# Three sets of four channel tiles by seven half products in block 6, and the sums of u queued behind the preceding block's last adds

## The chip, the cores and the metric

The kernel runs on one core of one Trainium2 chip. The metric is the device time of one execution in microseconds (us), lower is better. Engines are named as in the profile: PE (matrix products), DVE, ACT and POOL (elementwise work), SP (a queue that issues DMAs and DMA transposes). POOL issues DMAs too, the loads of q, k and v.

## The reference

Causal attention over 8 batches of 8 heads, 576 tokens and 16 beacon tokens in front, then a mixer over tokens of low rank, then two dense layers with a ReLU between them and a residual.

```
x = attention(q, k, v, beacon_k, beacon_v)        # B=8, S=576, H*D=512
h = x^T @ U @ V                                   # over tokens, rank 32
u = x + h^T
out = u + max(u @ w_ch1, 0) @ w_ch2               # 512 -> 2048 -> 512
```

## The kernel before

**Tiling.** Attention works on pairs of heads: pair `p` belongs to batch `p // 4`. Scores go to tiles `sps`, ACT turns them into weights (`expt`, by exp), DVE masks them against `bigmask`, PE makes the weighted sum `po`, DVE normalises it into `xb` (`rec`, then a multiply). When a batch is whole, its tokens are transposed into `uT` and the low-rank term is added. The two dense layers work on 9 blocks of 512 tokens, numbered 0 to 8, which run through batches: 4608 rows in all. A block is a list of units that goes into `queue`, and `fill(n)` takes n units from it between the pieces of attention. So a block's matmuls and the attention of a later batch alternate on PE, in an order that is written out by hand (`long_slot`), and blocks 7 and 8 run alone at the end. Every engine keeps the order in which the program emits its instructions.

**Layer 1** of a block makes 16 channel tiles of `gT` (128 channels by 512 tokens each). A plain tile (`layer_one`) is four matmuls of 512 columns into a bank `gps`, then a ReLU on ACT or DVE. A *set* (`quad` in the code) is four tiles, two of the lower eight and two of the upper eight, made at once by a scheme of Strassen's kind: seven half products in place of eight, each of four matmuls of 256 columns. `step(q, n)` emits set q in four steps, n = 0 to 3. It has a bank `qpsA` that gathers a running sum; after steps 0, 1 and 2 ACT copies that sum out (`copied`, into `kept` or a piece of a staging tile), and the next product of `qpsA` may start only when the copy has been taken. A second bank `qpsD` gathers too; after step 2 DVE adds it to a copy (`summed`), and only then may step 3 add its product to `qpsD`. A third, `qpsF`, is used within step 0. The set needs sums of pieces of w1 (`quad_weights`, four POOL instructions of 128x512, once) and sums of pieces of u (`u_sums`, four DVE instructions of 128x512 per block: t1 to t4, which lie in the last 512 columns of the four staging tiles `st`).

**Layer 2** is seven products of the same kind (`products`, banks `mpsA` to `mpsF`), each in two units (`c_unit`), and `after(k)` takes product k out of its bank with a DVE add; for the products on `mpsE` and at last on `mpsD` that add makes an output tile `ob`, to which POOL adds u (`residual`) before SP stores it. `ahead(n)` emits the sums of u of the next block within the last units of layer 2, one sum a unit from unit 10 on (`AHEAD`).

**Who uses what.** `PARTS` says how many sets a block makes: none in blocks 0 to 2, one in 3 to 6, three in 7 and 8 (`quads`). The four staging tiles hold q and k of a batch as loaded: `qk_tiles` gives even batches the first two and odd batches the other two; from batch 4 on (`DT0`) they are loaded by `load_whole` and brought into `kT` and `qT` by DMA transposes on SP (`turns`), one batch ahead. `coming` holds loads and weight builds that wait for their turn: each unit taken from `queue` lets one of them go to POOL. `pst` gives out the eight PSUM banks in the order in which they were emptied.

Of the kernel before, what the change touches and what calls it, by code (L numbers as in the profile page):

```python
# [11 lines left out]
F32 = mybir.dt.float32  # L12
# [18 lines left out]
def kernel(  # L31
# [14 lines left out]
    B, H, S, D = q.shape  # L46
# [6 lines left out]
    NH2 = H // 2  # L53
# [199 lines left out]

    def qk_tiles(b=0):

        t = staged[2 * (b % 2) : 2 * (b % 2) + 2]
        st = [x[:, :].rearrange("p (h e) -> p h e", h=H) for x in t]
        whole = [x[:, 0 : NT * DM].rearrange("p (j h d) -> p j h d", h=H, d=D) for x in t]
        return st, whole
# [311 lines left out]
    def quad_tiles(q):  # L571

        if q == 0:
            w = [pairs.tile([P, 512], F16, name=f"lw{k}", tag=f"pr{k % 2}") for k in range(4)]
        else:
            w = [staged[q - 1][:, ds(512 * k, 512)] for k in range(4)]
            f = staged[q + 1][:, 0 : 2048].bitcast(F32).rearrange("p (k i x) -> p k i x", k=2, i=2)
            lq["k", q] = (f[:, 0], f[:, 1], f[:, 0])
        lq["w", q] = [x.rearrange("p (c f) -> p c f", c=2) for x in w]

# [31 lines left out]
    def fast_units(t0, dst, last=False, parts=0, ahead=None):  # L612


        cell, banks, obs = {}, {}, {}
        quads = parts > 1
        cols = u_cols(t0, 512)

        def begin():
# [39 lines left out]
        def layer_one(dc, on_vector, between=lambda: None):  # L659

            g = pst([P, 512], F32, name="gps")
            for cc in range(NCC):
                for at, o, w in cols:
                    nc.tensor.matmul(  # L664
                        g[:, ds(o, w)], w1[:, cc, ts(dc, P)], uT[:, cc, ds(at, w)],
                        start=(cc == 0 and o == 0), stop=(cc == NCC - 1), skip_group_check=len(cols) > 1,
                    )
            between()
            if on_vector:
                nc.vector.tensor_scalar_max(out=cell["g"][:, dc, :], in0=g, scalar1=0.0)  # L670
            else:
                nc.scalar.activation(out=cell["g"][:, dc, :], in_=g, func=AF.Relu)  # L672
            emptying(g)

        def g_quads():
# [4 lines left out]
            held = {}  # L680

            def plain(k, dc):
                layer_one(dc, not quads and k in (2, 11, 13))

            def half(q, bank, a, b, fresh):
                if fresh:
# [32 lines left out]
            def step(q, n):  # L719
                d, e = 2 * q, HF + 2 * q  # L720
                if n == 0:
                    half(q, "A", of_w1(0, d), b11, True)
                    copied(q, 0)
                    half(q, "F", of_w1(2, d), b21, True)
                    summed(q, "F", 0, d, 0)
                    emptying(held.pop((q, "F")))
                    relu(cell["g"][:, ds(d, 2), 0:HT])
                elif n == 1:
                    half(q, "A", of_lw(q, 1), t2, False)
                    copied(q, 1)  # L730
                    half(q, "D", of_lw(q, 0), t1, True)
                elif n == 2:
                    half(q, "A", of_lw(q, 2), t3, False)
                    copied(q, 2)
                    summed(q, "D", 2, e, HT)
                else:
                    half(q, "A", of_w1(2, e), t4, False)
                    nc.scalar.activation(out=cell["g"][:, ds(e, 2), 0:HT], in_=held[q, "A"], func=AF.Relu)
                    emptying(held.pop((q, "A")))
                    half(q, "D", of_lw(q, 3), b22, False)  # L740
                    summed(q, "D", 1, d, HT)
                    emptying(held.pop((q, "D")))
                    relu(cell["g"][:, :, HT:512].rearrange("p (h d) t -> p h d t", h=2)[:, :, ds(d, 2), :])

            if not quads:
                slots = [2, (0, 0), 10, (0, 1), 3, 11, (0, 2), 4, (0, 3), 12, 5, 13, 6, 14, 7, 15]
                late = {11: ((0, 0, 4),), 12: ((1, 0, 4),), 13: ((2, 0, 4),), 14: ((0, 4, 3),), 15: ((1, 4, 3),)}
# [35 lines left out]

        after_g = {0: ((0, 6, 2), (1, 6, 2)), 1: ((2, 0, 4),), 4: ((2, 4, 4),), 6: ((3, 0, 4),), 7: ((3, 4, 4),)}
        sums_at = {k - NDC: x for k, x in SUMS.items()}
        if parts:
            sums_at = {0: ((2, 4, 3),), 1: ((0, 7, 1), (1, 7, 1)), 2: ((2, 7, 1), (3, 0, 4)), 3: ((3, 4, 4),)}

        b11, b21, b22 = w2[:, 0:HF, 0:HC], w2[:, HF:NDC, 0:HC], w2[:, HF:NDC, HC:DM]
# [112 lines left out]
        def c_unit(k, j):  # L902
            p = pieces(products[k][0])[j]
            if parts and k < 2:
                (first, second_on)[k](*p)
            else:
                product(*products[k], *p)
            for x in sums_at.get(2 * k + j, ()):
                sums(*x)
            for u in ahead(2 * k + j) if ahead else ():  # L910
                u()
            if j == 1 and not (parts and k < 2):
                after(k)

        def chain_units():

# [296 lines left out]
    DT0 = 4  # L1213
    LAG = 10
    HINT = 5
    FAST = 1
    PARTS = {3: 1, 4: 1, 5: 1, 6: 1, 7: 3, 8: 3}
    AHEAD = 10
    SUMS = {
# [27 lines left out]

    def sums_ahead(t):

        if PARTS.get(t, 0) != 1:  # L1250
# [64 lines left out]
    with tc.manual_schedule(engines={ENG.PE, ENG.Activation, ENG.DVE, ENG.SP, ENG.Pool}):  # L1315
# [186 lines left out]

        for p in range(NP1, NP):
            b, c = divmod(p, NH2)
            if c == (1 if b >= DT0 else 0) and b + 1 < B:
                load_batch(b + 1)
            if p == P6 + 3:
                quad_tiles(0)
                coming.extend(quad_weights(0))
            if p == NP - 3:  # L1510
                for n in (1, 2):
                    quad_tiles(n)
                    coming.extend(quad_weights(n))
            if c == (1 if b + 1 == DT0 else 2) and DT0 <= b + 2 < B:
                load_whole(b + 2)
            qk = qkT_of(p + 2) if P6 <= p and p + 2 < min(NP, DT0 * NH2) else []
            if p == P6:
                turn_x(b - 1)
                mix_between(b - 1)
            if c == 0 and DT0 <= b + 1 < B:  # L1520
                tr = turns(b + 1)
                fill_turns(tr, len(tr))
            if p < P6:
                play(third[c])
            else:
                long_slot(p, c, av_of(p), qk or [lambda: None] * 2)
# [109 lines left out]
```

## Time and profile before

| what | value |
| --- | --- |
| time, median of 3 runs | 334.12 us (333.8 to 334.57) |
| the profiled execution's own time, its span | 334.53 us, 332.9 us |
| PE, DVE, ACT, POOL busy | 324.4, 264.9, 195.8, 149.3 us |
| layer 1 of block 6 on PE | 249.01 to 265.16 us |
| layer 2 of block 6 | 265.16 to 278.46 us |
| layer 1 of block 7 (three sets, no attention beside it) | 278.46 to 291.12 us |

The time from a row of a timeline is its start in the span, then the time from its first start to its last end; "x8" means eight instructions that follow each other. Ends of matmuls are modelled, so the step from one start to the next says what a matmul costs on PE. A pair in brackets is the idle time ahead of the instruction and what ended it.

### The profile page before, as it was taken

To read this page: it belongs to the slowest core of one execution; us is meant where nothing else is said; L and a number is where in the kernel's file an instruction comes from. 1 tells how busy PE (TensorE), PEld (TensorE's weight loads), DVE (VectorE), ACT (ScalarE), POOL (GpSimd) and SP (SyncE) were. 2 spreads that over 40 slices of the span, in tenths; PEclk is the share of its full clock that TensorE was granted. 3 is DMA by queue.
4 is the path that set the end of the run, shared out by engine and by line. 5 is a ranking of instruction groups with operands and counts; after the bars stand their busy time and mean duration, and the time that the engine had idled before them with its cause. 6 is when DMAs were issued, how large, how long until landed. Compare 5 with 4: busy or idle time off the path is not lost.

```text
span 332.9 us, 9194 instructions
## 1 busy us (share of the span) xinstructions
PE 324.4 (97%) x3646; PEld 226.9 (68%) x3646; DVE 264.9 (80%) x600; ACT 195.8 (59%) x429; POOL 149.3 (45%) x185
## 2 busy tenths in 40 slices
PE   7999999999999999999999999999999999999994
PEld 3665555555578655876588888764886588788784
DVE  6685888678898667796789777887799858898993
ACT  5966971688972577347844695379535413713710
POOL 8986824657147950669046903360294014010010
PEclk9999999999999999999999999999999999999999
DMA  7999999999999995999989995964204413205013
GB/s 161 143 165 153 177 188 199 193 188 170 79 128 165 208 140 76 130 184 145 124 146 181 141 147 104 129 143 109 41 33 142 77 46 109 51 32 141 20 36 101
DMA packets 150562, 41.99 MB, mean 126 GB/s; under 512 B 131312, under 2 KB 149936, under 8 KB 150512
## 3 DMA queue, kind: packets, MB, share of 16 engines
q0 software_dynamic: 87568, 18.18, 75.0%
q1 hardware_dynamic: 62144, 22.41, 35.4%
q10 hardware_dynamic: 800, 0.75, 0.7%
q8 instruction: 30, 0.49, 0.6%
q14 instruction: 20, 0.16, 0.2%
HBM read 37.45 MB, written 9.44 MB: 141 GB/s over the span
## 4 chain that ended last, share of the span: by engine, by line
PE 86%; DVE 6%; ACT 5%; DMA 1%; issue 1%; DVEq 0%
PE gps L664 21%; PE mpsA L880 8%; PE po L428 8%; PE sps L410 6%; PE mpsD L800 5%; PE qpsA L690 5%; PE cps L1019 4%; PE gps L993 4%; PE mpsB L800 3%; PE mpsE L800 3%; PE mpsC L800 3%; PE qpsD L690 3%; PE mpsF L800 2%; PE mpsD L880 2%; ACT expt L377 2%; ACT w L377 2%
## 5 line engine op out<-in xcount | busy, mean ns | idle before, releaser
L419 ACT ACTIVATE expt<-sps 128x496 f16<-128x496 f32 (+2 forms) x192 | 82.2, 546 | 43.7 <-PE sps L410 43.7
L820 POOL TENSOR_TENSOR ob<-ob,ut 128x512 f32<-128x512 f32 x26 | 31.9, 1230 | 137.5 <-DVE ob L820 66.1
L664 PE MATMUL gps<-uT,w 128*128 128x512 f16 (+1 forms) x400 | 84.9, 354 | 0.2 <-ACT kT L1145 0.2
L800 PEld LDWEIGHTS <-gT 128*128 128x128 f16 x576 | 54.3, 98 | 8.7 <-issue 2.6
L664 PEld LDWEIGHTS <-w 128*128 128x128 f16 x400 | 36.6, 98 | 29.0 <-issue 1.8
L672 ACT ACTIVATE gT<-gps 128x512 f16<-128x512 f32 x68 | 40.6, 618 | 19.6 <-PE gps L664 14.1
L642 DVE TENSOR_TENSOR gT<-gT 128x1024 f16<-128x1024 f16 (+3 forms) x90 | 47.3, 550 | 0.9
L239 POOL DMA_DIRECT2D vs<-in_v_dram x50 | 40.0, 813 | 14.8 <-DMA w<-in_moe_w_ch_dram 12.0
L428 PEld LDWEIGHTS <-expt 128*128 128x128 f16 x900 | 33.8, 98 | 8.5 <-issue 1.5
L428 PE MATMUL po<-vs,expt 128*128 128x65 f16 x900 | 36.4, 194 | 0.3
L349 DVE TENSOR_TENSOR expt<-expt,bigmask 128x768 f16<-128x768 f16 x54 | 34.5, 679 | 0.4 <-ACT expt L419 0.2
L880 PEld LDWEIGHTS <-gT 128*128 128x128 f16 x336 | 31.2, 98 | 4.2
L437 DVE TENSOR_TENSOR xb<-po,rec 128x320 f16<-128x320 f32 x64 | 31.4, 491 | 2.2
L709 ACT ACTIVATE kept<-qpsA 128x512 f32<-128x512 f32 x18 | 10.8, 602 | 22.6 <-PE qpsA L690 12.0
L410 PE MATMUL sps<-qT,kT 64*128 64x80 f16 (+4 forms) x288 | 22.9, 281 | 0.2 <-DVE ob L820 0.2
L670 DVE TENSOR_SCALAR gT<-gps 128x512 f16<-128x512 f32 x20 | 13.8, 689 | 11.4 <-PE gps L664 11.3
L436 DVE RECIPROCAL rec<-po 128x5 f32<-128x5 f32 x64 | 12.0, 188 | 12.1 <-PE po L428 11.7
L377 ACT ACTIVATE expt<-sps 128x496 f16<-128x496 f32 (+2 forms) x48 | 20.5, 556 | 1.3 <-PE sps L371 1.3
L410 PEld LDWEIGHTS <-kT 64*128 64x128 f16 x288 | 10.3, 94 | 13.2 <-issue 8.6
L880 PE MATMUL mpsA<-w,gT 128*128 128x256 f16 x160 | 19.0, 273 | 0.0
L1092 POOL DMA_DIRECT2D st<-in_k_dram x20 | 16.9, 859 | 1.3 <-DVE qT L332 1.3
L1092 POOL DMA_DIRECT2D st<-in_q_dram x20 | 16.9, 875 | 0.0
(159 smaller groups left out, 519.1 us busy)
## 6 DMA issues: line engine op xcount, KB each, us to landing
out_dram<-ob SPq DMA_DIRECT2D x33, 256.0 KB, 3.2
vs<-in_v_dram POOLq DMA_DIRECT2D x18, 128.0 KB, 7.1
w<-in_moe_w_ch_dram POOLq DMA_DIRECT2D x4, 512.0 KB, 6.8
w<-in_moe_w_ch_dram POOLq DMA_DIRECT2D x2, 1024.0 KB, 12.9
st<-in_k_dram POOLq DMA_DIRECT2D x12, 128.0 KB, 6.2
st<-in_q_dram POOLq DMA_DIRECT2D x12, 128.0 KB, 7.6
st<-in_k_dram POOLq DMA_DIRECT2D x4, 288.0 KB, 12.0
st<-in_q_dram POOLq DMA_DIRECT2D x4, 288.0 KB, 12.8
```

Source lines behind the costliest of these rows:

```text
L239: nc.gpsimd.dma_start(out=dst[a : a + nq[j], j, :, :], in_=src[hs, ds(q0[j], nq[j]), :].rearrange("h p d -> p h d"))
L349: nc.vector.tensor_tensor(out=e, in0=e, in1=bigmask[:, :, :].rearrange("p (a b) x -> p a b x", b=2), op=ALU.min)
L377: nc.scalar.activation(out=ex[i][:, ds(AT[g], gw[g])], in_=ps[g, i][:, 0 : gw[g]], func=AF.Exp, scale=scale)
L410: nc.tensor.matmul(banks[i][:, ds(at0 + o, w)], kT(hp, c, ch), qT[hp, c, ds(qa, w)], start=True, stop=True, skip_group_check=len(unit) > 1,)
L419: nc.scalar.activation(out=at[p][3][i][:, ds(AT[g], gw[g])], in_=bank[:, ds(at0, gw[g])], func=AF.Exp, scale=scale)
L428: nc.tensor.matmul(po[:, j, :], ex[0 : nk[c], ds(blk[(c, j)], P)], vs[0 : nk[c], ds(c * H * E + h * E, E)], start=(c == 0), stop=(c == j),)
L642: nc.vector.tensor_tensor(out=o[:, ds(d0, n)], in0=x[:, ds(d0, n)], in1=y[:, ds(d0, n)], op=op)
L664: nc.tensor.matmul(g[:, ds(o, w)], w1[:, cc, ts(dc, P)], uT[:, cc, ds(at, w)], start=(cc == 0 and o == 0), stop=(cc == NCC - 1), skip_grou ...
L672: nc.scalar.activation(out=cell["g"][:, dc, :], in_=g, func=AF.Relu)
L800: nc.tensor.matmul(ps, a()[:, d, ds(P * i, P)], bm[:, d, ds(c0, w)], start=fresh and d == 0 and i == 0, stop=d == HF - 1, skip_group_check ...
L880: nc.tensor.matmul(ps, a()[:, d, ds(P * i, P)], bm[:, d, ds(c0, w)], start=fresh and d == 0, stop=d == HF - 1, skip_group_check=True,)
L1092: coming.append(lambda d=dst, s=src, a=m[j] - nq[j], n=m[j], j=j: nc.gpsimd.dma_start(out=d[a:n, j, :, :], in_=s[:, ds(q0[j], nq[j]), :].r ...
```

## The change

Block 6 makes three sets and four plain tiles in layer 1 instead of one set and twelve plain tiles. Its order of units is new, the bank `qpsD` of sets 1 and 2 is begun a step later than that of set 0, and the sums that layer 2 needs are emitted mostly in layer 2. For that the w1 sums of set 1 are built by POOL in the second pair of batch 4 instead of at the end of batch 7, and live in the third staging tile; the copies of set 1 go to the first. That takes the third and fourth staging tile from the batches, so all batches from 4 on are loaded into the first two, and batch 5 is loaded one pair later. Last, in layer 2 of every block of this kind `after(k)` is emitted ahead of `ahead(n)`, so that a sum of u stands behind the add of the same unit instead of ahead of it.

```diff
     def qk_tiles(b=0):
-        t = staged[2 * (b % 2) : 2 * (b % 2) + 2]
+        i = 2 * (b % 2) if b < DT0 else 0
+        t = staged[i : i + 2]
...
-            w = [staged[q - 1][:, ds(512 * k, 512)] for k in range(4)]
-            f = staged[q + 1][:, 0 : 2048].bitcast(F32).rearrange("p (k i x) -> p k i x", k=2, i=2)
+            w = [staged[q + 1][:, ds(512 * k, 512)] for k in range(4)]
+            f = staged[q - 1][:, 0 : 2048].bitcast(F32).rearrange("p (k i x) -> p k i x", k=2, i=2)
...
-        quads = parts > 1
+        quads = t0 // 512 >= NBLK - 2
...
-                layer_one(dc, not quads and k in (2, 11, 13))
+                layer_one(dc, parts == 1 and k in (2, 11, 13))
...
+                elif n == 1 and parts > 1 and not quads:
+                    if q == 0:
+                        half(q, "D", of_lw(q, 0), t1, True)
+                    half(q, "A", of_lw(q, 1), t2, False)
+                    copied(q, 1)
...
                     copied(q, 2)
+                    if q and not quads:
+                        half(q, "D", of_lw(q, 0), t1, True)
                     summed(q, "D", 2, e, HT)
...
-                slots = [2, (0, 0), 10, (0, 1), 3, 11, (0, 2), 4, (0, 3), 12, 5, 13, 6, 14, 7, 15]
+                if parts > 1:
+                    slots = [
+                        (0, 0), (0, 1), 6, (0, 2), (1, 0), (0, 3), (1, 1), 14, (1, 2), (2, 0), (1, 3), (2, 1), 7,
+                        (2, 2), 15, (2, 3),
+                    ]
+                    late = {12: ((0, 0, 4),), 14: ((1, 0, 4),)}
...
-        if parts:
+        if parts > 1:
+            sums_at = {
+                0: ((0, 4, 4),), 1: ((1, 4, 4),), 2: ((2, 0, 4),), 3: ((2, 4, 4),), 4: ((3, 0, 4),), 5: ((3, 4, 4),),
+            }
+        elif parts:
...
+            if j == 1 and not (parts and k < 2):
+                after(k)
             for u in ahead(2 * k + j) if ahead else ():
                 u()
-            if j == 1 and not (parts and k < 2):
-                after(k)
...
-    PARTS = {3: 1, 4: 1, 5: 1, 6: 1, 7: 3, 8: 3}
+    PARTS = {3: 1, 4: 1, 5: 1, 6: 3, 7: 3, 8: 3}
...
+            if p == P6 + NH2 + 1:
+                quad_tiles(1)
+                coming.extend(quad_weights(1))
...
-                for n in (1, 2):
-                    quad_tiles(n)
-                    coming.extend(quad_weights(n))
-            if c == (1 if b + 1 == DT0 else 2) and DT0 <= b + 2 < B:
+                quad_tiles(2)
+                coming.extend(quad_weights(2))
+            if c == 2 and DT0 <= b + 2 < B:
                 load_whole(b + 2)
```

On DVE, where layer 2 of block 5 ends (`st_113` to `st_116` are written with t1 to t4 of block 6, `expt` is masked for the two heads whose weighted sums come next). Before:

```order
L820 TENSOR_TENSOR ob<-mpsD,kept 128x512
L593 TENSOR_TENSOR st_113<-uT 128x512
L593 TENSOR_TENSOR st_114<-uT,st_113 128x512
L820 TENSOR_TENSOR ob<-mpsE,kept 128x512
L349 TENSOR_TENSOR expt_105<-expt_105,bigmask 128x3x2x128
L349 TENSOR_TENSOR expt_106<-expt_106,bigmask 128x3x2x128
L593 TENSOR_TENSOR st_115<-uT 128x512
L593 TENSOR_TENSOR st_116<-uT,st_114 128x512
L820 TENSOR_TENSOR ob<-mpsD,kept 128x512
```

The same place of DVE with the change:

```order
L839 TENSOR_TENSOR ob<-mpsD,kept 128x512
L594 TENSOR_TENSOR st_113<-uT 128x512
L839 TENSOR_TENSOR ob<-mpsE,kept 128x512
L594 TENSOR_TENSOR st_114<-uT,st_113 128x512
L350 TENSOR_TENSOR expt_105<-expt_105,bigmask 128x3x2x128
L350 TENSOR_TENSOR expt_106<-expt_106,bigmask 128x3x2x128
L594 TENSOR_TENSOR st_115<-uT 128x512
L839 TENSOR_TENSOR ob<-mpsD,kept 128x512
L594 TENSOR_TENSOR st_116<-uT,st_114 128x512
```

The second sum now stands between the add of `mpsE` and the two masks, and the last add stands ahead of the fourth sum. The same rows stand at the ends of blocks 2, 3 and 4.

On ACT in layer 1 of block 6 (a row with `gps` is a plain tile's ReLU, one with `kept<-qpsA` or `st<-qpsA` is the copy of a set's running sum, `gT<-qpsA` its last ReLU, `expt` the exp of scores). Before:

```order
L672 ACTIVATE gT<-gps 128x512
L709 ACTIVATE kept<-qpsA 128x512
L419 ACTIVATE expt_107<-sps_4849 128x496
L419 ACTIVATE expt_108<-sps_4850 128x496
L709 ACTIVATE kept<-qpsA 128x512
L672 ACTIVATE gT<-gps 128x512 x2
L709 ACTIVATE kept<-qpsA 128x512
L672 ACTIVATE gT<-gps 128x512
L738 ACTIVATE gT<-qpsA 128x2x256
L672 ACTIVATE gT<-gps 128x512 x5
```

The same place of ACT with the change:

```order
L710 ACTIVATE kept<-qpsA 128x512 x2
L673 ACTIVATE gT<-gps 128x512
L420 ACTIVATE expt_107<-sps_4854 128x496
L420 ACTIVATE expt_108<-sps_4855 128x496
L710 ACTIVATE kept<-qpsA 128x512
L710 ACTIVATE st_113<-qpsA 128x512
L746 ACTIVATE gT<-qpsA 128x2x256
L710 ACTIVATE st_113<-qpsA 128x512
L673 ACTIVATE gT<-gps 128x512
L710 ACTIVATE st_113<-qpsA 128x512
L710 ACTIVATE st_114<-qpsA 128x512
L746 ACTIVATE gT<-qpsA 128x2x256
```

Before, the second copy of the one set stood behind the two exps. Now it is the third copy of set 0, with a plain tile's ReLU ahead of the exps, and the copies of set 1 follow it.

On POOL, in the part of the program that belongs to batch 4 (`lw` are the w1 sums of set 0, those into `st_115` the w1 sums of set 1, `vs` loads of v, `ob` the residual of an output tile), with the change:

```order
L1111 DMA st_114<-in_q_dram 80x8x64
L606 TENSOR_TENSOR lw_2404<-w_93 128x512
L606 TENSOR_TENSOR lw_2405<-lw_2404,w_93 128x512
L606 TENSOR_TENSOR lw_2406<-w_93 128x512
L606 TENSOR_TENSOR lw_2407<-w_93,lw_2405 128x512
L606 TENSOR_TENSOR st_115<-w_93 128x512
L839 TENSOR_TENSOR ob<-ob,ut 128x512
L606 TENSOR_TENSOR st_115<-st_115,w_93 128x512
L606 TENSOR_TENSOR st_115<-w_93 128x512
L606 TENSOR_TENSOR st_115<-w_93,st_115 128x512
L221 DMA vs_112<-in_beacon_v_dram 16x8x64
```

Before, `lw_2412<-w_93,lw_2410` was followed at once by the load of `vs_112`, and the eight sums of sets 1 and 2 stood together near the end of batch 7.

More of the change, by code (lines that the diff above doesn't have):

```diff
@@ L745, in g_quads @@
             if not quads:
-                slots = [2, (0, 0), 10, (0, 1), 3, 11, (0, 2), 4, (0, 3), 12, 5, 13, 6, 14, 7, 15]
-                late = {11: ((0, 0, 4),), 12: ((1, 0, 4),), 13: ((2, 0, 4),), 14: ((0, 4, 3),), 15: ((1, 4, 3),)}
+                if parts > 1:
[4 more added lines that the diff above has]
+                    late = {12: ((0, 0, 4),), 14: ((1, 0, 4),)}
+                else:
+                    slots = [2, (0, 0), 10, (0, 1), 3, 11, (0, 2), 4, (0, 3), 12, 5, 13, 6, 14, 7, 15]
+                    late = {11: ((0, 0, 4),), 12: ((1, 0, 4),), 13: ((2, 0, 4),), 14: ((0, 4, 3),), 15: ((1, 4, 3),)}
                 def unit(k, slot):
@@ L1248, in sums_ahead @@
     def sums_ahead(t):
-        if PARTS.get(t, 0) != 1:
+        if t not in PARTS or t >= NBLK - 2:
             return None
```

## The prediction

> **What bounds the kernel now.** I read the page first, for shares and clock.
>
> ```profile
> span 332.9 us, 9194 instructions
> PE 324.4 (97%) x3646; PEld 226.9 (68%) x3646; DVE 264.9 (80%) x600; ACT 195.8 (59%) x429; POOL 149.3 (45%) x185
> PE 86%; DVE 6%; ACT 5%; DMA 1%; issue 1%; DVEq 0%
> ```
>
> PE is busy for 97% of the span, and 86% of the chain that ended last is PE. So an edit is worth what it takes from PE's stream, plus the waits in that stream that it ends, less those that it makes. A windows view gives the stretches that matter: layer 1 of block 6, then layer 1 of block 7, which already makes three sets (columns: length, busy time of PE, PEld, DVE, ACT, POOL, then clock, DMA share, GB/s).
>
> ```profile
> 249.01:265.16 16.15, 15.98 (x145) 9.48 (x142) 13.90 (x27) 8.04 (x15) 3.98 (x3) 1.00 0.48 106
> 278.46:291.12 12.66, 12.66 (x102) 9.71 (x100) 10.63 (x21) 8.63 (x15) 1.72 (x2) 1.00 0.39 106
> ```
>
> PE runs at full clock in both. In block 6 it has a hole, and DVE is busy for 13.90 of 16.15 us: it is second. PE's timeline shows the hole between a plain tile and the scores behind it; the two rows after the dots are the same place in block 5.
>
> ```profile
> 251.66 1.03 PE L664 MATMUL gps<-uT,w 128*128 128x512 f16 x4
> 252.62 0.31 PE L410 MATMUL sps<-qT,kT 64*128 64x336 f16 x1
> 253.10 0.37 PE L410 MATMUL sps<-qT,kT 64*128 64x336 f16 x5 [0.17 <-DVE ob L820]
> ...
> 218.44 0.60 PE L410 MATMUL sps<-qT,kT 64*128 64x336 f16 x8
> 218.97 0.61 PE L690 MATMUL qpsA<-st,lw 128*128 128x256 f16 x4
> ```
>
> From the first score matmul to the second, 0.48 us pass. In block 5 eight of them take 0.53 us together, 0.07 each on average, so about 0.45 us are a wait, more than the 0.17 in brackets, since modelled ends cover the rest. What PE waits for is DVE's last `ob` add of block 5, which frees a bank. DVE and POOL show why it was late:
>
> ```profile
> 247.87 0.68 DVE L820 TENSOR_TENSOR ob<-mpsE,kept 128x512 f32<-128x512 f32 x1
> 248.47 2.34 DVE L349 TENSOR_TENSOR expt<-expt,bigmask 128x768 f16<-128x768 f16 x2
> 250.73 1.38 DVE L593 TENSOR_TENSOR st<-uT 128x512 f16<-128x512 f16 x1
> 252.04 0.41 DVE L593 TENSOR_TENSOR st<-uT,st 128x512 f16<-128x512 f16 x1
> 252.37 0.68 DVE L820 TENSOR_TENSOR ob<-mpsD,kept 128x512 f32<-128x512 f32 x1
> ...
> 248.93 1.47 POOL L605 TENSOR_TENSOR st<-w,st 128x512 f16<-128x512 f16 x1
> 250.36 1.47 POOL L820 TENSOR_TENSOR ob<-ob,ut 128x512 f32<-128x512 f32 x1
> ```
>
> The same DVE instruction takes 0.41 us at 252.04 and 1.38 us at 250.73. The long one lies over a POOL instruction. POOL is then building w1 sums and adding residuals.
>
> **The change, part by part.** *Fewer columns.* A matmul's price is the step between starts in block 7:
>
> ```profile
> 283.74 0.60 PE L690 MATMUL qpsA<-st,lw 128*128 128x256 f16 x4
> 284.18 1.04 PE L690 MATMUL qpsA<-st,st 128*128 128x256 f16 x8
> 285.05 1.89 PE L664 MATMUL gps<-uT,w 128*128 128x512 f16 x8
> 286.78 0.49 PE L690 MATMUL qpsA<-st,w 128*128 128x256 f16 x3
> ```
>
> Twelve of 256 columns take 285.05 - 283.74 = 1.31 us, 0.109 each; eight of 512 take 1.73 us, 0.216 each. Four plain tiles are 16 x 0.216 = 3.46 us, a set is 28 x 0.109 = 3.05 us. Two sets more save **0.82 us**. This lies on the path whole. The Trainium skill speaks against it ("TensorE: Matmul & The Clock Gate", Back-to-back issue gap): a stream of weight loads and matmuls runs at about 81 ns for 128 columns and 131 ns for 512. On a line between these, an estimate from that page, 256 columns cost 98 ns, and a set of 2.73 us would be dearer than four tiles of 2.10 us: the sum's first term would be +1.3 us. The rows above disagree with that, and they decide.
>
> *The wait at 252.62.* With the change four of POOL's eight late builds are gone from there, and the last add stands ahead of a sum. I take the wait as gone: **-0.45 us**. What is late next is below.
>
> *A new wait of PE for ACT.* By the order of ACT in block 6, PE's units after the first plain tile are six score matmuls, step 2 of set 0, step 0 of set 1, step 3 of set 0. Step 3 needs the copy from step 2, and that copy stands behind a ReLU and two exps. ACT's rows (the last two from block 6 before):
>
> ```profile
> 284.38 0.60 ACT L709 ACTIVATE kept<-qpsA 128x512 f32<-128x512 f32 x1 [0.28 <-PE qpsA L690]
> 284.87 1.08 ACT L709 ACTIVATE st<-qpsA 128x512 f32<-128x512 f32 x2
> 286.11 0.60 ACT L672 ACTIVATE gT<-gps 128x512 f16<-128x512 f32 x1 [0.16 <-PE gps L664]
> 253.49 1.06 ACT L419 ACTIVATE expt<-sps 128x496 f16<-128x496 f32 x2 [1.92 <-PE sps L410]
> 254.43 0.60 ACT L709 ACTIVATE kept<-qpsA 128x512 f32<-128x512 f32 x1
> ```
>
> The plain tile's matmuls that began at 285.05 end their turn at 285.92; its ReLU starts 0.19 later. The next instruction follows 0.49 after a ReLU or copy (284.38 to 284.87), two exps take 0.94 (253.49 to 254.43), a copy 0.60. So the copy is done 0.19 + 0.49 + 0.94 + 0.60 = 2.22 us after the tile. PE meanwhile has six scores (0.53 less two of 496 columns at 0.11 each, about 0.31), four matmuls of step 2 (0.44) and eight of step 0 (0.87): 1.62. It waits **+0.60 us**. In the old order two plain tiles lay in that gap.
>
> *A wait for DVE behind it.* Step 3's second product needs the DVE add of step 2, which needs the same copy.
>
> ```profile
> 256.71 0.59 ACT L709 ACTIVATE kept<-qpsA 128x512 f32<-128x512 f32 x1
> 257.34 0.69 DVE L712 TENSOR_TENSOR gT<-qpsD,kept 128x512 f16<-128x512 f32 x1 [0.57 <-ACT kept L709]
> ```
>
> The add starts 0.04 after the copy and takes 0.69: 0.73 us, with 0.44 of PE's step 3 beside it. Wait: **+0.30 us**. The like places of sets 1 and 2 have cover. Behind step 2 of set 1 lie a weighted sum and step 0 of set 2, behind that of set 2 a plain tile of 0.87 us, which covers copy (0.60) and add (0.69) only with the first product's 0.44 as well. I put **+0.10 us** there, between 0 and 0.3.
>
> *The sums of u.* The second sum now delays the masks of the next two heads by 0.41 us at the ends of blocks 2 to 5. Block 4's start shows what that meets:
>
> ```profile
> 179.66 1.98 DVE L349 TENSOR_TENSOR expt<-expt,bigmask 128x768 f16<-128x768 f16 x2
> 180.12 1.51 DVE L349 TENSOR_TENSOR expt<-expt,bigmask 128x768 f16<-128x768 f16 x1
> 179.82 1.40 POOL L820 TENSOR_TENSOR ob<-ob,ut 128x512 f32<-128x512 f32 x1 [1.26 <-DVE ob L820]
> 181.40 0.61 PE L428 MATMUL po<-vs,expt 128*128 128x65 f16 x15
> 219.17 4.01 POOL L820 TENSOR_TENSOR ob<-ob,ut 128x512 f32<-128x512 f32 x3 [8.49 <-DVE xb L437]
> ```
>
> The first mask runs before POOL's residual of the same output tile, the second waits for it and ends at 181.63, 0.41 after POOL. With the sum in front, the first mask is the one that waits. POOL starts when the sum is done, 179.66 + 0.41 = 180.07, 0.13 earlier than before, so the mask ends near 181.5, and the weighted sum due at 181.40 waits; with the weight load between, about 0.2 us, from 0 to 0.45. The Trainium skill has this as a rule ("SBUF — State Buffer", Who interferes with whom): DVE with two inputs from SBUF and a POOL instruction that reads SBUF hold a shared port as an exclusive lock, and issue order decides who blocks. By that rule the order that the change makes is the worse one, and these rows agree. Block 5 is spared: POOL stands still there until 219.17. Block 6 meets it, since with POOL's builds gone its residual falls as in block 4. Block 3 may, but POOL is then behind with the moved loads and builds; I count 0 there. Two places: **+0.40 us**.
>
> *Loads and builds.* Batch 5 is loaded a pair later, and four builds of 1.16 us each stand in POOL ahead of v of that batch.
>
> ```profile
> st<-in_q_dram POOLq DMA_DIRECT2D x12, 128.0 KB, 7.6
> 109.61 1.80 POOL L1092 DMA_DIRECT2D st<-in_q_dram  x2
> 131.30 2.30 SPq L1108 DMA_TRANSPOSE kT<-st  x1
> ```
>
> Before, POOL issued loads of q from 109.61 on, 0.9 us each. In the new order nine loads stand behind a residual that came after all of them, at about 115; so the last is issued near 123, an estimate, and lands 7.6 later, near 131, as the transposes of batch 5 begin. Batch 5 is scored two pairs after these. I put 0 here; without that cover SP would hold stores and transposes for a microsecond or two.
>
> *Sum*, against the profiled execution's own 334.53 us (332.9 of span, 1.63 around it): -0.82 - 0.45 + 0.60 + 0.30 + 0.10 + 0.40 = +0.13. That execution is 0.41 above the median of the runs, so I add 0.13 to the median of 334.12: 334.25, written **334.3**. A measurement of this kernel tells about 0.2%, 0.67 us, from no change, so the forecast is no change within that.
>
> **The rivals.** *A: the copy does not hold PE.* For it: block 7 makes three sets in 12.66 us with PE busy throughout, and gains of 1.27 us would then stand alone: 334.12 - 1.27 = 332.9. Against it: block 7 has no exps, and the 0.60 comes from fixed orders on two engines. Chance 0.12; over half of the new waits must vanish to be faster by 0.2%.
>
> *B: DVE is still late.* The rows behind its last `ob` add price the adds and weighted sums that follow:
>
> ```profile
> 252.97 0.18 DVE L436 RECIPROCAL rec<-po 128x5 f32<-128x5 f32 x1
> 253.59 0.68 DVE L712 TENSOR_TENSOR gT<-qpsF,kept 128x512 f16<-128x512 f32 x1
> 254.31 0.29 DVE L717 TENSOR_SCALAR gT<-gT 128x512 f16<-128x512 f16 x1
> 254.52 0.18 DVE L436 RECIPROCAL rec<-po 128x5 f32<-128x5 f32 x1
> ```
>
> By starts, a weighted sum's two instructions take 0.62, an add with its ReLU 0.72 + 0.21. The second mask ends some 1.5 us into block 6 (the first 1.0 in, as in block 4, the second half a microsecond later); two sums of u at 0.33 (252.04 to 252.37), the `ob` add at 0.60, add and ReLU, two weighted sums: 1.5 + 0.66 + 0.60 + 0.93 + 1.24 = 4.9. The add behind the copy is due later: PE's work ahead of the first plain tile is as long as before, the tile starts at 251.66 and ends 0.87 on, the copy is done 2.22 after that, 5.7 us into the block. So DVE has 0.8 us in hand. Before, its last `ob` add began 3.4 us into the block, in my count 1.8. If it stays those 1.6 us late, the 0.45 stays and the add is 0.8 late, less where the waits overlap: 334.25 + 0.95 = 335.2, an estimate. For it: 13.90 busy of 16.15, six adds more, and the port. Against: half of POOL's builds leave. Chance 0.25.
>
> *C: half products do not overlap as full ones do.* At their full rows a group of four costs 0.60 (283.74) and a plain tile 1.03 (251.66): a set of 4.20 against four tiles of 4.12, so two sets lose 0.16 in place of gaining 0.82, and the time is 334.25 + 0.82 + 0.16 = 335.2. The skill's gap figures above point this way. The twelve in 1.31 us, in a block of sets alone, speak against it. Chance 0.02.
>
> *D: late loads hold SP*, 1 to 2 us, chance 0.03.
>
> **How the numbers follow.** The forecast has 0.58, of which 0.56 lie within 0.2% and 0.01 on either side. Of B's 0.25, 0.23 are slower by more than that. Faster: 0.12 + 0.01 = 0.13. Slower: 0.01 + 0.23 + 0.02 + 0.03 = 0.29. Same: the rest, 0.58. The range goes from half-way to A, 333.4, to just beyond B, 335.4.
>
> **What would show it.** Right: PE's timeline in block 6 with a hole of about 0.6 us ahead of step 3 of set 0, ended by ACT's `kept`, and one of 0.3 ended by DVE; no hole at the scores; a hole of 0.2 at the first `po` of blocks 4 and 6; layer 1 of block 6 about 16.0 us long. Wrong: layer 1 of block 6 at 15.0 us (A), DVE's last `ob` add more than 3 us into it (B), or a wait on SP's transposes near 131 us (D).

## The result, and the profile after

The changed kernel takes 335.76 us (median of 9 runs, 335.08 to 336.83), the kernel before beside it 334.25 us (9 runs, 333.80 to 334.76). The ratio is 1.0047, 95% interval 1.0035 to 1.0059: slower by 1.5 us, where the forecast was 0.13 us and the range ended at 335.4. The profiled execution took 335.72 us, that of the kernel before 334.53. Medians are over all runs; ratios and intervals leave out the few runs in the chip's slower state.

From the page of the changed kernel, the span, the engines' shares and the chain that ended last:

```profile
span 334.0 us, 9275 instructions
PE 324.9 (97%) x3670; PEld 228.6 (68%) x3670; DVE 266.2 (80%) x604; ACT 197.4 (59%) x432; POOL 149.3 (45%) x185
PE 87%; ACT 6%; DVE 3%; DMA 1%; issue 1%; ACTq 0%; DVEq 0%
```

DVE's part of the chain fell from 6% to 3%, and yet the span grew. So shares don't show it; stretches do. The windows view of layer 1 of blocks 6 and 7 (length, busy time of PE, PEld, DVE, ACT, POOL, then clock, DMA share, GB/s):

```profile
249.85:265.75 15.90, 15.38 (x169) 11.65 (x166) 14.40 (x30) 9.70 (x19) 1.83 (x2) 1.00 0.37 91
279.05:291.71 12.66, 12.66 (x102) 9.70 (x100) 10.62 (x21) 8.64 (x15) 1.72 (x2) 1.00 0.40 106
```

Block 6, where the new sets are, got shorter: 15.90 us, 16.15 before. Its rows on PE, then ACT, then DVE show the forecast's steps one by one:

```profile
252.68 1.03 PE L665 MATMUL gps<-uT,w 128*128 128x512 f16 x4
253.64 0.39 PE L411 MATMUL sps<-qT,kT 64*128 64x336 f16 x6
253.96 0.61 PE L691 MATMUL qpsA<-st,lw 128*128 128x256 f16 x4
...
254.85 0.60 PE L691 MATMUL qpsF<-uT,w 128*128 128x256 f16 x4
255.84 0.60 PE L691 MATMUL qpsA<-st,w 128*128 128x256 f16 x4 [0.39 <-ACT kept L710]
256.56 0.60 PE L691 MATMUL qpsD<-uT,lw 128*128 128x256 f16 x4
...
254.24 1.05 ACT L420 ACTIVATE expt<-sps 128x496 f16<-128x496 f32 x2
255.17 0.62 ACT L710 ACTIVATE kept<-qpsA 128x512 f32<-128x512 f32 x1
...
255.82 0.69 DVE L713 TENSOR_TENSOR gT<-qpsD,kept 128x512 f16<-128x512 f32 x1 [0.84 <-ACT kept L710]
```

The six scores at 253.64 follow at once: no hole there. Four matmuls of 256 columns take 0.44, so step 3 of set 0 was due at 255.29 and starts at 255.84, 0.55 late, behind ACT's copy; its second product was due at 256.28 and starts at 256.56, 0.28 late, behind DVE's add.

So the loss lies ahead of block 6. I took the start of each matmul in both traces and subtracted; the difference is flat nearly everywhere and steps at a few places. The table gives the steps for the changed kernel and for every experiment (us, by which PE falls back against the trace of before; "po" is a block's first weighted sum, "plain" the plain tile behind the scores; layer 1 of block 6 includes its own first `po`).

| kernel | po, block 3 | plain, block 3 | po, block 4 | plain, block 4 | scores, block 5 | layer 1, block 6 | elsewhere after 100 us |
|---|---|---|---|---|---|---|---|
| changed | 0.76 | 0.11 | 0.17 | 0.16 | 0.29 | -0.25 | 0 |
| e1 order only | 0.18 | 0.16 | 0.17 | 0.16 | 0 | +0.31 | 0 |
| e10 second sum only | 0.18 | 0 | 0.17 | 0 | 0 | +0.31 | 0 |
| e11 fourth sum only | 0 | 0 | 0 | 0 | 0 | -0.34 | 0 |
| e3 loads only | 0 | 0.03 | 0 | 0 | 0 | -0.47 | 0.19 at 158 |
| e2 old order | 0 | 0.06 | 0 | 0 | 0 | -0.42 | 0.19 at 157 |
| e6 change, builds later | 0.18 | 0.17 | 0.17 | 0.16 | 0 | -0.25 | 0.44 at 162 |
| e7 no residual | 0 | 0 | 0 | 0 | 0 | -0.42 | 0.09 at 158 |
| e8 sum behind masks | 0 | 0.72 | 0 | 0.33 | 0 | -0.42 | 0 |
| e4 new slots | 0 | 0.31 | 0 | 0 | 0.79 | -1.19 | 0.09, 0.19 |
| e5 and builds later | 0 | 0 | 0 | 0 | 0 | -1.19 | 0.62 at 162 |
| e9 and builds split | 0 | 0 | 0 | 0 | 0 | -1.20 | 0.51 at 192 |
| e12 split, earlier | 0 | 0 | 0 | 0 | 0 | -1.19 | 1.20 at 124 |

In the changed kernel blocks 3 to 5 lose 1.49 and block 6 gains 0.25: a loss of 1.24 us, where the medians are 1.5 apart and the two profiled executions 1.19. (In the first 20 us the other traces are 0.32 to 1.00 ahead of before's, whatever the kernel, e3's loses 0.47 again before 60 us, and behind the last matmul they lose 0.05 to 1.38; none of this is put down to a change.)

The largest step, on PE, DVE and POOL at block 3; the last three rows are PE and DVE at the same place before:

```profile
145.69 1.03 PE L665 MATMUL gps<-uT,w 128*128 128x512 f16 x4
147.31 0.62 PE L429 MATMUL po<-vs,expt 128*128 128x65 f16 x15 [0.59 <-DVE expt L350]
...
144.82 0.41 DVE L594 TENSOR_TENSOR st<-uT,st 128x512 f16<-128x512 f16 x1
145.16 2.57 DVE L350 TENSOR_TENSOR expt<-expt,bigmask 128x768 f16<-128x768 f16 x2
...
143.85 1.79 POOL L239 DMA_DIRECT2D vs<-in_v_dram  x2
145.66 1.17 POOL L839 TENSOR_TENSOR ob<-ob,ut 128x512 f32<-128x512 f32 x1
...
146.34 1.03 PE L664 MATMUL gps<-uT,w 128*128 128x512 f16 x4
147.21 0.61 PE L428 MATMUL po<-vs,expt 128*128 128x65 f16 x15
145.47 1.98 DVE L349 TENSOR_TENSOR expt<-expt,bigmask 128x768 f16<-128x768 f16 x2
```

The second sum of u is done at 145.23. The first mask, which takes 0.55 alone, starts at 145.16 and ends at about 147.26 (the two take 2.57): it waits for POOL's residual, and not only while that runs (145.66 to 146.83) but already while it stands behind the late loads of v (143.85 to 145.64). That the residual holds it, and not the loads, is what e7 shows below.

### The profile page after: what moved, and what is told of

It reads as the page before. It is cut to its first block, busy times and chain, and to the rows that moved or that the text cites. A ratio compares the mean times of both kernels' runs of the same rounds, so it can differ in the third digit from the quotient of the medians.

```text
span 334.0 us, 9275 instructions
## 1 busy us (share of the span) xinstructions
PE 324.9 (97%) x3670; PEld 228.6 (68%) x3670; DVE 266.2 (80%) x604; ACT 197.4 (59%) x432; POOL 149.3 (45%) x185
## 4 chain that ended last, share of the span: by engine, by line
PE 87%; ACT 6%; DVE 3%; DMA 1%; issue 1%; ACTq 0%; DVEq 0%
PE gps L665 19%; PE mpsA L899 8%; PE po L429 8%; PE qpsA L691 6%; PE mpsD L819 6%; PE sps L411 6%; PE cps L1038 4%; PE gps L1012 4%; PE mpsE L819 3%; PE qpsD L691 3%; PE mpsC L819 3%; PE mpsB L819 3%; ACT expt L378 2%; PE mpsF L819 2%; PE mpsD L899 2%; ACT w L378 2%
## 5 line engine op out<-in xcount | busy, mean ns | idle before, releaser
L665 PE MATMUL gps<-uT,w 128*128 128x512 f16 (+1 forms) x368 | 77.8, 351 | 0.2 <-ACT kT L1164 0.2
L643 DVE TENSOR_TENSOR gT<-gT 128x1024 f16<-128x1024 f16 (+3 forms) x87 | 50.5, 603 | 1.0
L665 PEld LDWEIGHTS <-w 128*128 128x128 f16 x368 | 33.4, 98 | 25.9 <-issue 1.8
L673 ACT ACTIVATE gT<-gps 128x512 f16<-128x512 f32 x63 | 37.8, 619 | 16.0 <-PE gps L665 11.5
L350 DVE TENSOR_TENSOR expt<-expt,bigmask 128x768 f16<-128x768 f16 x54 | 33.3, 656 | 0.4 <-ACT expt L420 0.2
L671 DVE TENSOR_SCALAR gT<-gps 128x512 f16<-128x512 f32 x17 | 11.7, 687 | 8.8 <-PE gps L665 8.7
```

The costliest lines, as they stand in the source:

```text
L350: nc.vector.tensor_tensor(out=e, in0=e, in1=bigmask[:, :, :].rearrange("p (a b) x -> p a b x", b=2), op=ALU.min)
L643: nc.vector.tensor_tensor(out=o[:, ds(d0, n)], in0=x[:, ds(d0, n)], in1=y[:, ds(d0, n)], op=op)
L665: nc.tensor.matmul(g[:, ds(o, w)], w1[:, cc, ts(dc, P)], uT[:, cc, ds(at, w)], start=(cc == 0 and o == 0), stop=(cc == NCC - 1), skip_grou ...
```

## The experiments

### The order of sums and adds: e1, e10, e11

All three are the kernel before with only the order changed: e1 in the whole, e10 only for `k == 5` (the second sum), e11 only for `k == 6` (the fourth).

```diff
+            if j == 1 and not (parts and k < 2):
+                after(k)
             for u in ahead(2 * k + j) if ahead else ():
                 u()
-            if j == 1 and not (parts and k < 2):
-                after(k)
```

> The kernel before, with only the order of c_unit changed: the sum of u behind the block's add, in all blocks; loads, builds and block 6 are those of before. Theory 1, the new order is what costs in blocks 3 to 5: behind the sum, the first mask is the one that waits for POOL's residual, so the first weighted sum and then the whole DVE queue run late. In the trace of the changed kernel PE fell back against before by 0.17 + 0.16 in block 4 and 0.29 in block 5, and by 0.74 + 0.11 in block 3, where late v loads come on top; with loads as before block 3 should lose what block 4 does, 0.33, and block 6's start 0.15. So about 0.33 + 0.33 + 0.29 + 0.15 = +1.1, 335.3 us. Theory 2, the loads and builds that come later on POOL are what costs and the order is nearly free: +0.2, 334.4 us.

> The kernel before, with only the second sum of u behind its add (the one ahead of the masks); the fourth stays ahead of the last add. Theory: this sum alone makes the first mask wait for POOL's residual, so the holes at the first weighted sums of blocks 3, 4 and 6 stand as with the whole order (0.16, 0.16, 0.67, less 0.46 at block 6's scores), and those at the plain tile (0.16 twice) are smaller or gone: 334.05 + 0.55 = 334.6 us. Rival: both sums are needed for the loss, 334.1 us.

> The kernel before, with only the fourth sum of u behind the last add. Theory: the masks are untouched, so no hole at the first weighted sums; at the plain tile behind at most the 0.16 of blocks 3 and 4, from the ReLU that took 0.71 instead of 0.29: 334.05 to 334.4 us. Rival: the loss of the order sits in this sum, 335.0 us.

Measured: e1 335.19 us against 334.07, ratio 1.0037 (1.0023 to 1.0050). e10 334.65 against 334.10, 1.0019 (1.0010 to 1.0029). e11 333.63 against 334.10, 0.9987 (0.9975 to 0.9999).

So the order alone costs 1.1 us, and theory 2 of e1 falls, though not every place came as I had put it: block 5 lost nothing, and block 6's first weighted sum came 0.67 late and not 0.15, its second lost 0.10 more, and the scores behind them gave back 0.47. The second sum, behind the add that POOL's residual follows, makes the cost, as forecast for e10. The fourth sum, which I had expected to cost a little, is a small gain, only just clear of no change. In e1, at block 3 (PE, DVE, POOL), the collision without late loads:

```profile
145.49 1.03 PE L664 MATMUL gps<-uT,w 128*128 128x512 f16 x4
146.53 0.63 PE L428 MATMUL po<-vs,expt 128*128 128x65 f16 x15
...
144.63 0.41 DVE L593 TENSOR_TENSOR st<-uT,st 128x512 f16<-128x512 f16 x1
144.96 1.98 DVE L349 TENSOR_TENSOR expt<-expt,bigmask 128x768 f16<-128x768 f16 x2
...
144.79 1.26 POOL L820 TENSOR_TENSOR ob<-ob,ut 128x512 f32<-128x512 f32 x1 [1.29 <-DVE ob L820]
...
149.47 0.71 DVE L717 TENSOR_SCALAR gT<-gT 128x512 f16<-128x512 f16 x1
```

A first weighted sum starts 0.87 behind its plain tile where nothing waits (before: 146.34 to 147.21); here 1.04. The last row is a ReLU further down DVE's queue; it comes into play below. In e11 DVE's last add of block 5 comes first, and of the hole at PE's scores 0.13 is left: from the first of the six to what follows it takes 0.45, in the changed kernel 253.96 - 253.64 = 0.32 (DVE, then PE):

```profile
251.28 0.68 DVE L820 TENSOR_TENSOR ob<-mpsD,kept 128x512 f32<-128x512 f32 x1
251.88 0.41 DVE L593 TENSOR_TENSOR st<-uT,st 128x512 f16<-128x512 f16 x1
...
250.90 1.03 PE L664 MATMUL gps<-uT,w 128*128 128x512 f16 x4
251.86 0.52 PE L410 MATMUL sps<-qT,kT 64*128 64x336 f16 x6
252.31 0.61 PE L690 MATMUL qpsA<-st,lw 128*128 128x256 f16 x4
```

The two halves do not add up (+0.55 and -0.47 against +1.12), and the table says why: the 0.16 at the plain tile needs both sums late (0.32 over blocks 3 and 4), and the hole at block 6's scores can be won only once.

The rows on DVE show what meets at the plain tile. Its bank comes free with DVE's normalising multiply (`xb`), and ahead of that stands a ReLU, the last row of e1 above. Where the fourth sum stands behind the last add (the changed kernel, e1, e6, e8, e11), this ReLU began 0.3 us into a load that POOL was issuing, in blocks 3 and 4 both, and took 0.65 to 0.72 instead of 0.29. Only e7 has that order without this: there a residual is left out, the ReLU began later in a load and took 0.31 to 0.34. In e10 it took 0.29 and no plain tile was late. In e11 it took 0.71, and at block 3 the multiply ended at 150.53, just ahead of the plain tile's start at 150.59. In e1 the queue was late by the second sum as well, and the tile waited. So neither the late queue nor the long ReLU is enough.

### What the masks wait for: e7, e8

Of the two edits below, the first is e7's and the second e8's:

```diff
-                residual("21", 1, 0)
+                store("21", 1, 0) if ahead else residual("21", 1, 0)
...
-            return us[n - AHEAD : n - AHEAD + 1] if n >= AHEAD else []
+            return us[slice(*{10: (0, 1), 12: (1, 3), 13: (3, 4)}.get(n, (0, 0)))]
```

> The changed kernel without POOL's residual add for output tile 21 in blocks 2 to 5 (the sum with u is left out there; the tile is stored as DVE leaves it). Theory: the masks wait for this POOL instruction, not for the sum's own 0.41 us; without it both masks take 0.55 and the holes at the first weighted sums of blocks 3, 4 and 6 (0.74, 0.17, 0.15) go: 335.76 - 1.06 = 334.7 us. Rival: the sum's own time makes the masks late; the holes stay, 335.7 us.

> The changed kernel with the second sum of u moved behind the two masks (one unit later); the fourth sum stays behind the last add as in the change. Theory: the first mask is again ahead of POOL's residual, so the holes at the first weighted sums go (1.06 in all), and those at the plain tile behind (0.11 in block 3, 0.16 in block 4), which belong to the fourth sum, stay: 334.7 us. Rival: any sum of u behind an add costs what it does wherever it stands, 335.5 us.

Measured: e7 334.16 against 334.03, ratio 1.0007 (0.9992 to 1.0023); e8 335.20, 1.0031 (1.0019 to 1.0043). In e7 the sum still stands ahead of the masks (DVE), POOL issues loads of v beside both masks, and PE's first weighted sum is on time:

```profile
145.21 0.42 DVE L594 TENSOR_TENSOR st<-uT,st 128x512 f16<-128x512 f16 x1
145.54 1.02 DVE L350 TENSOR_TENSOR expt<-expt,bigmask 128x768 f16<-128x768 f16 x2
...
144.25 2.52 POOL L239 DMA_DIRECT2D vs<-in_v_dram  x3
...
146.08 1.03 PE L665 MATMUL gps<-uT,w 128*128 128x512 f16 x4
146.94 0.61 PE L429 MATMUL po<-vs,expt 128*128 128x65 f16 x15
```

Without the one POOL instruction the two masks take 1.02 instead of 2.57 and all holes of blocks 3 and 4 go, those at the plain tile too: neither the sum's own 0.41 nor the loads were what held the masks. The time is 0.5 below the forecast 334.7, since the plain tiles (0.27) and block 5 (0.29) lose nothing either. e8 was half right, and its time came nearer to the rival's 335.5. No first weighted sum is late, but now the second mask waits for the residual (the two take 2.41), three sums stand between it and the multiply, one more than before, the ReLU takes 0.65 again, and the plain tile pays:

```profile
147.63 0.68 DVE L839 TENSOR_TENSOR ob<-mpsD,kept 128x512 f32<-128x512 f32 x1
148.24 0.41 DVE L594 TENSOR_TENSOR st<-uT,st 128x512 f16<-128x512 f16 x1
...
149.91 0.65 DVE L718 TENSOR_SCALAR gT<-gT 128x512 f16<-128x512 f16 x1
150.68 0.49 DVE L438 TENSOR_TENSOR xb<-po,rec 128x320 f16<-128x320 f32 x1
...
151.23 1.04 PE L665 MATMUL gps<-uT,w 128*128 128x512 f16 x4 [0.54 <-DVE xb L438]
```

### Loads and builds: e3, e2, e6

e3 is the changed kernel with the old order and `PARTS[6]` at 1, e2 with the old order alone, e6 with the builds of set 1 moved only:

```diff
-            if p == P6 + NH2 + 1:
+            if p == P6 + 2 * NH2:
                 quad_tiles(1)
                 coming.extend(quad_weights(1))
```

> The kernel before with only the moved loads of batch 5 and the moved builds of set 1 (one set in block 6, old slots, old order of sums and adds). Theory 1: late v loads meet no mask that waits, 334.2 to 334.5 us. Theory 2: +0.7 to +1.0, about 335.1 us, with a hole at block 3's first weighted sum near 147 us.

> The changed kernel, with the sum of u put ahead of the add again. Theory 1: what was lost in blocks 3 to 5 (1.47 in the two traces) and the 0.15 at block 6's first weighted sum come back; the gain of 0.82 in columns and the waits of 0.55 and 0.28 in block 6 stay; the old wait of 0.45 at the scores stays away if POOL's builds caused it: 335.8 - 1.5 = 334.2 us, between 334.0 and 334.5 with that wait back. Theory 2: block 3 still loses 0.7, and the time stays near 335.0 to 335.3 us.

> The changed kernel with nothing but the four builds of set 1 moved three pairs later. Theory: POOL's late v loads add to the new order at block 3, where PE waited 0.74 instead of the 0.16 of the order alone; with POOL on time the wait falls to 0.16, so 335.76 - 0.6 = 335.2 us. Rival: the 0.74 has nothing to do with POOL's lateness: 335.8 us.

Measured: e3 333.99 against 334.07, ratio 0.9997 (0.9988 to 1.0006); e2 334.15, 1.0002 (0.9976 to 1.0027); e6 335.54 against 334.03, 1.0038 (1.0026 to 1.0050). e2 came as its first theory had it, and e3 a little below. The moved loads and builds cost nothing that can be measured in the old order. With the new order they matter at one place: with the builds out of POOL's way the step at block 3 is 0.18 instead of 0.76. This is read from the traces: e6's time lies between its two forecasts, and its ratio, 1.0038 after 1.0047, is not shown to be lower. In its trace the builds fall on two other masks, at 162 us (0.44 there). The 0.19 near 158 us in e2, e3 and e4 and the 0.09 in e7 are the ReLU again: one of 128x1024, ahead of another multiply, takes 0.70 (in e7 0.61) instead of 0.43 beside a load.

### Towards a better version: e4, e5, e9, e12

e4 is e2 with other slots in block 6; e5, e9 and e12 move its builds of set 1 as well (e5 as in e6; e9 two to pair P6 + 2 * NH2 and two to P6 + 3 * NH2; e12 two left where they are and two to P6 + 2 * NH2).

```diff
-  (0, 0), (0, 1), 6, (0, 2), (1, 0), (0, 3), (1, 1), 14, (1, 2), (2, 0), ...
+  (0, 0), (0, 1), (1, 0), (0, 2), 6, (1, 1), 14, (0, 3), (1, 2), (2, 0), ...
```

> The changed kernel with the old order of sum and add, and with other slots in block 6: steps (0,0), (0,1), (1,0), (0,2), then plain tile 6, (1,1), plain tile 14, (0,3), (1,2) and on as in the change, so that between step 2 and step 3 of set 0 PE has 6 x 0.22 + ... = two plain tiles and a step more to do. If the two waits of block 6 (0.55 for ACT's copy, 0.28 for DVE's add) come from too little work of PE between those steps, they go: 0.8 less than the changed kernel with the old order alone, about 333.4 us, below before. If DVE is what is late in block 6 in any order (rival B of the prediction), the holes only move, and the time is that of the old order alone.

> The kernel with old order and new slots, and the four builds of set 1 moved three pairs later, to about 158 us, where POOL stands still in the traces (159.6 to 171.2 in the changed kernel). If the moved builds, by putting POOL behind at block 3, are what ate the gain of the new slots (PE lost 0.30 at 151.6 and 0.19 at 158.2 in that run), the time is 0.3 to 0.5 below it: 333.3 to 333.5 us. Rival: the loss there is in the moved loads, or comes from the transposes of k that land just in time at block 5 (0.78 there in that run), and nothing is gained: 333.8 us.

> The kernel with old order, new slots in block 6, and the four builds of set 1 in two pairs, one behind the loads at about 157 us and one behind those at about 191 us, where in the last trace DVE has no fast two-input work beside them (there the third and fourth build held two masks, and PE waited 0.59 at 162 us). If the builds' collisions are what is left, PE loses nothing in blocks 3 to 5 and gains 1.2 in block 6: 334.05 - 1.2 = 332.9 us, and with what the transposes of k cost at block 5 in some executions up to 333.5. Rival: the spread of the single times (333.5 to 336.2 with the builds later) comes from somewhere else, and the median stays at 334.

> Old order, new slots in block 6, and the four builds of set 1 in two pairs: two where the change has its first, ahead of v of batch 5, and two behind the loads at about 157 us, where two builds cost PE nothing in the last such trace. What is left out is the pair at 191 us (0.49 there) and two of the four that held up v of batch 5. Theory: PE then gains its 1.2 in block 6 and gives back at most 0.2 to 0.3 at block 3: 334.1 - 1.0 = 333.1 us, and 333.5 with the spread that the kernels with these loads had. Rival: the spread, not the collisions, makes the median, and it stays at 333.8.

Measured: e4 333.83 against 334.07, ratio 0.9998 (0.9984 to 1.0011); e5 334.53 against 334.03, 1.0014 (1.0000 to 1.0029); e9 333.85 against 334.10, 0.9999 (0.9987 to 1.0011); e12 334.63 against 334.35, 1.0009 (0.9981 to 1.0036). None is shown faster: e4 missed its 333.4, and for the other three the rivals, that the median would stay where it was, came nearer than the theories. Yet block 6 gained 1.19 or 1.20 in all four traces, nearly the 0.82 and 0.45 of the forecast without the new waits, so DVE is not what is late there (rival B of the prediction). Each trace loses at some other place where a POOL instruction or a late transfer meets DVE or PE: 1.38 in e4 and 1.20 in e12, as much as block 6 gains, but only 0.62 in e5 and 0.51 in e9, whose profiled executions (333.52 and 333.43) were among the faster ones. In e5 (POOL, DVE, PE):

```profile
160.37 1.60 POOL L606 TENSOR_TENSOR st<-w,st 128x512 f16<-128x512 f16 x1
160.88 1.97 DVE L350 TENSOR_TENSOR expt<-expt,bigmask 128x768 f16<-128x768 f16 x2
162.45 0.63 PE L429 MATMUL po<-vs,expt 128*128 128x65 f16 x15 [0.44 <-ACT expt L420]
```

In e12 it is a build of set 0, in code that e4 has as well. First e12's DVE, POOL and PE, then e4's DVE and POOL at the same place:

```profile
120.87 2.66 DVE L643 TENSOR_TENSOR gT<-gT 128x1024 f16<-128x1024 f16 x1
121.76 1.21 POOL L606 TENSOR_TENSOR lw<-w 128x512 f16<-128x512 f16 x1
124.21 2.76 PE L665 MATMUL gps<-uT,w 128*128 128x512 f16 x12 [1.02 <-DVE xb L438]
...
121.17 1.44 DVE L643 TENSOR_TENSOR gT<-gT 128x1024 f16<-128x1024 f16 x1
122.05 1.57 POOL L606 TENSOR_TENSOR lw<-w 128x512 f16<-128x512 f16 x1
```

In one execution DVE waits out POOL's build and takes 2.66; in the other it takes 1.44, ends ahead of the build, and the build takes 1.57. PE lost 1.20 at this place in the first; in the second it lost nothing here and 0.09 at 133 us. That the medians come from such chances is what the traces suggest; it was not tested by taking the builds away. The best version that the runs show is e11: 333.63 us, 0.13% below before (interval 0.01% to 0.25%). That is one of thirteen comparisons and only just clear of no change.

## Why the prediction was wrong, point by point

- **Fewer columns, -0.82, and the wait at the scores, -0.45**: right. With the new waits taken out (e4, e5, e9, e12) block 6 gains 1.19 of 1.27. The rule of the Trainium skill ("TensorE: Matmul & The Clock Gate", Back-to-back issue gap) by which the first term would have been +1.3, and rival C with it, are out; in block 6, too, four matmuls of 256 columns take 0.44, 0.11 each. The wait at the scores goes for either of two reasons: builds moved (e3, -0.47) or the add ahead of the sum (e11, -0.34); the prediction put both to it at once.
- **The wait for ACT, +0.60, and for DVE's add, +0.30**: right, 0.55 and 0.28. **Ends of sets 1 and 2, +0.10**: no step there. Layer 1 of block 6 was forecast at about 16.0 and took 15.90. The first `po` of block 6 was 0.16 late (0.2 forecast).
- **The sums of u, +0.40 for two places**: this is the step that failed. Its mechanism was right, shown by e7, and its size at block 4 too (0.17 for 0.2). Three things were wrong. Block 3 was counted at 0 because POOL would be behind there; being behind made it the worst place, 0.76, since a residual that stands ready behind POOL's own load issues holds the mask longer (0.18 with POOL on time, e6). Second, I stopped at the first mask. DVE's queue is late behind it, a ReLU in that queue meets a load issue of POOL (0.65 and 0.71 instead of 0.29), and the plain tile that waits for the multiply behind both comes 0.11 and 0.16 later; the prediction had asked who waits for the mask and not who waits for what stands behind it. Third, the term was bounded by 0.45 a place, from the row at block 4; the row that could have warned stood in the trace of before and was not read. On DVE and POOL there:

```profile
110.83 2.19 DVE L349 TENSOR_TENSOR expt<-expt,bigmask 128x768 f16<-128x768 f16 x2
109.61 1.80 POOL L1092 DMA_DIRECT2D st<-in_q_dram  x2
111.42 1.18 POOL L820 TENSOR_TENSOR ob<-ob,ut 128x512 f32<-128x512 f32 x1
```

  The second of these masks was due when the first was done, at about 111.3, ahead of the residual's start at 111.42, and still waited it out: 2.19 for the two.
- **Loads and builds, 0**: right as a term of its own (e3), wrong as a term that stands alone, by the above. **Scores of block 5**: not in the prediction. PE's queue stands there on semaphores that SP's transposes raise (the bracket of e4's row names ACT, which had long been done), and the median transpose of q took longest to land where the step was largest. The medians are close (7.8 in e3 and e10, without a wait); single transposes say it better. The fourth of q landed 1.33 us after the start of the plain tile ahead of the scores in the changed kernel and 1.82 after it in e4, and the scores went on 0.13 later; in the other twelve traces it landed at 1.02 or earlier and nothing waited. The medians, from the changed kernel, then e4:

```profile
qT<-st SPq DMA_TRANSPOSE x5, 7.9
...
qT<-st SPq DMA_TRANSPOSE x5, 8.4
```

  Steps of 0.29 and 0.79; in the trace of before the same row has 7.1 and there is no such wait. This differs between executions of the same code up to there (e2 and e4), so I put it to chance, which is not shown; what makes a transpose land late stays open.
- **Rivals**: A's gain of 1.27 in block 6 exists, but only with the new slots. B's and C's 335.2 came nearest to the measured time, by mechanisms that did not occur: DVE's last `ob` add, by B more than 3 us into block 6, began 1.70 into it (251.55 in a block that starts at 249.85), and C's price is answered above. D's wait did not come: PE has no step near 131 us.

In sum the working forecast -0.82 - 0.45 + 0.60 + 0.30 + 0.10 + 0.40 = +0.13; the trace has block 6 at -0.25 (forecast -0.07 with its `po`), and blocks 3 to 5 at +1.49 where +0.20 was forecast.

## What to carry to other kernels

Where DVE and POOL share work, ask of every reordering which of them is now issued first: a short instruction put ahead of a ready one can hold that one for the whole length of a POOL instruction, not for its own. Follow the delay down the queue to the next thing that a later instruction frees, and don't count an engine that is behind as harmless: what is queued on it holds others for longer. Split a reordering into its single moves before judging it; here one half cost 0.55 us and the other gained 0.47.

## What the runs showed of the hardware that I had not expected

- *A POOL instruction holds DVE before its recorded start.* After 100 us, the 14 traces have 152 masks and sums of u that began while POOL was issuing a load with no tensor instruction behind it in reach; each took 0.41 to 0.56 us. In twelve more cases the next POOL instruction was a tensor one that was free to go, 0.02 to 0.50 us ahead of its recorded start, and DVE took 1.5 to 2.1 us. It ended 0.4 us behind POOL (masks) or 0.3 (sums), nearly its whole own time, so it had done next to nothing before POOL started. (In two more, in e11, POOL's next instruction still waited for DVE, and the sum took 0.41.) In layer 2's sums the lead can be longer: e12's at 120.87 began 0.89 ahead of the build. What held e4's at 121.17, which took 1.44 and ended ahead of the build, is open. The Trainium skill ("SBUF — State Buffer", Who interferes with whom) says that whoever issues first has the shared ports for the whole instruction; the traces agree, and here "first" was earlier than the start that the profile records. Whether the hold begins early or the recorded start is late can't be told from them.
- *A load issue on POOL also holds a ReLU on DVE.* The ReLU of 128x512 f16 takes 0.29 us. Where it began about 0.3 us into a load issue it took 0.65 to 0.72; where it began 0.07 into one, 0.29. In e7 it began 0.64 and 0.67 into one and took 0.31 and 0.34. The ReLU of 128x1024 (0.43) is of a piece: 0.70 when begun 0.47 into a load issue, 0.52 at 0.66, 0.47 at 0.72, and 0.43 at 0.22 or earlier. (One in e9, with a POOL build coming behind the load, took 1.03.) So all that a load held ended as if they had begun 0.65 to 0.76 us into the load issue: only a part of it holds DVE. The row in the changed kernel at block 4, on DVE and POOL:

```profile
184.72 0.71 DVE L718 TENSOR_SCALAR gT<-gT 128x512 f16<-128x512 f16 x1
184.43 1.79 POOL L1111 DMA_DIRECT2D st<-in_k_dram  x2
```

  The same section says that a TENSOR_SCALAR can take both of DVE's port pairs, and it infers that a load that POOL issues needs the write side of the shared pair for its descriptors, which a two-input instruction does not take. That fits both kinds of row; no run here separated them further.
